# Decode attention block in fp32: output weights in two loads of 24 and 8 heads, the last values between them, all heads joined in one way, the mean taken from row sums

## Chip, core and metric

One core of a Trainium2 chip runs one launch of the kernel. The metric is the time on the device in microseconds. TensorE (PE), VectorE (DVE), ScalarE (ACT), GpSimd (POOL) and SyncE (SP) run their own instruction streams and wait for each other through semaphores; 16 DMA engines fill the on-chip memory.

## What is computed

One decode step, batch 2, model width 512, 32 heads of 128, a cache of 8192 keys and values for each head, all in fp32: a layer norm, attention over the cache with the output weights `wo`, the residual, a second layer norm, and a two-layer network with a squared ReLU.

```python
def _A_ref(x, k_cache, v_cache, wq, wo):
    q = (x @ wq).reshape(B, Sq, H, Dh).transpose(0, 2, 1, 3)
    scores = jnp.einsum("bhqd,bhkd->bhqk", q, k_cache) * (Dh ** -0.5)
    p = _softmax(scores, axis=-1)
    o = jnp.einsum("bhqk,bhkd->bhqd", p, v_cache)
    return o.transpose(0, 2, 1, 3).reshape(B, Sq, H * Dh) @ wo
...
h = x + _A_ref(_layernorm(x), k_cache, v_cache, wq, wo)
h2 = h + _B_ref(_layernorm(h), w1, b1, w2, b2)      # relu(z @ w1 + b1) ** 2 @ w2 + b2
```

## The kernel before

**Streaming.** The 64 pairs of head and batch element (pair number = 2 x head + batch element) are streamed through three buffers `ring[0..2]` of 8 MB, each holding a pair's keys (first half) and values (second half). All loads of this kind are issued by SP in program order (`load`, L122); SP waits for a semaphore `FREE` before it refills a buffer, and DVE gives it when it is through with the buffer. For each pair PE multiplies keys with the query (`front`, L234) into PSUM tiles `s[0..2]`, in two halves of 4096 keys; DVE takes maxima (`maxes`, stored negated in `nm`), ACT exponentials with their sums (`exps`, into `ls`), and DVE multiplies values with the exponentials and sums along the row (`product`, L252, eight a pair, into `ac`). Maxima are local to a partition row and a half; the rows are put on one scale at the end.

**The tail** (L139 on) begins when the last pair (63, so head 31 of batch element 1) is loaded. Its keys go into the first half of `ring[0]` with a semaphore of their own (`LK`). Then SP loads the output weights `WO` (8 MB, `ring[1]`) at once, the last values in five pieces (`V_PIECES`, in eighths), and, when `ring[2]` is free, `W1` in two pieces (three quarters and one quarter of its rows) and `W2` in four. `take` (L60) is the wait for a load, `after` (L54) the wait for another engine's result; a wait stands in the stream of the engine that waits, and everything behind it on that engine waits too.

**Joining.** `stats` (L287) gives each pair the minimum of its negated maxima over all rows and the factor `wt` for each of them, `sums` and `invert` the reciprocal of the softmax denominator `rl`, `folded` (L317) the weighted sum over the rows. In the kernel before this runs for 62 pairs (31 heads) first; DVE writes the joined outputs, each 16 times repeated, into `big` (L337), PE multiplies them with `WO` (L344, two passes a head, four column groups), ACT copies the sum into `acc` (L348), and PE folds the four groups and turns the result to features on partitions (L351). DVE's program has this order behind it: products 0 to 2 of the last pair, the addition of that result to `hT` (L366), a second `stats` for head 31, products 3 and 4, `sums`, product 5, `invert`, products 6 and 7. Then head 31 is joined alone: `folded`, `o31` (L379), PE with its block of `WO` (L382), an addition to `hT` (L385).

**The rest.** `centre` (L176) takes the mean over features with a DVE sum, a PE product with `ones_d` and a DVE subtraction into `xc`; `xr` (L387) is the input of W1, which PE multiplies in the order of its pieces (L396). After the first piece `spread` (L186) makes the variance and its root. DVE transposes the result, scales it, adds `b1` and squares; PE adds `h + b2` through the identity (L405) and W2's products (L421) into one PSUM tile, which DVE copies (L426) and SP stores (L428).

Of the kernel before, what the change touches and what calls it, by code (L numbers as in the profile page):

```python
# [27 lines left out]
W1_PIECES = [3, 1]  # L28
V_PIECES = [(0, 2), (2, 4), (4, 6), (6, 7), (7, 8)]
# [34 lines left out]
def attention_block_kernel(nc, small, kvd, wqd, kld, vld, wod, w1d, w2d, out):  # L64
# [32 lines left out]
    o31 = sbuf("o31", B)  # L97
    xr = sbuf("xr", DB, 16, B)
    hT = sbuf("hT", DB, B)
# [15 lines left out]
    SM, LK = p.sem("small"), p.sem("k63")  # L115
    LV = [p.sem(f"v63_{k}") for k in range(len(V_PIECES))]
# [59 lines left out]
    def centre(src, tok, bank):  # L176
        p.after("dve", tok)
        tok = p.tell("dve", dve.tensor_reduce(part, src.rearrange("p d b -> p b d"), axis=AX.X, op=ALU.add))  # L178
        p.after("pe", tok)
        tok = p.tell("pe", pe.matmul(bank[:, :B], ones_d, part, start=True, stop=True))  # L180
        p.after("dve", tok)
        tok = p.tell("dve", dve.tensor_tensor(xc, src, bank[:, None, :B].to_broadcast([P, DB, B]), op=ALU.subtract))
        p.after("dve", tok)
        return tok

    def spread(bank):  # L186
        tok = p.tell("dve", dve.tensor_tensor(sq, xc, xc, op=ALU.mult))
        p.after("dve", tok)
        tok = p.tell("dve", dve.tensor_reduce(part, sq.rearrange("p d b -> p b d"), axis=AX.X, op=ALU.add))
# [5 lines left out]
        tok = p.tell("dve", dve.reciprocal(rstd, rstd))  # L195
        return tok
# [3 lines left out]
    tok = centre(xT, t_c, pm[0])  # L200
    tok = spread(pm[1])
# [83 lines left out]
    t_m = p.tell("dve", dve.tensor_copy(hT, xT))  # L285

    def stats(lo, nb):  # L287
        n2 = slice(lo * NC, (lo + nb) * NC)
        p.after("pe", t_m)
        for j in range(NQ):  # L290
            ins = pe.matmul(pm[0][:, j * nb * NC : (j + 1) * nb * NC], pick[:, j, :], nm[:, n2], start=True, stop=True)  # L291
        tok = p.tell("pe", ins)
        p.after("dve", tok)
        tok = p.tell("dve", dve.tensor_reduce(gm[:, lo : lo + nb], pm[0][:, : NQ * nb * NC].rearrange(  # L294
            "p (j i c) -> p i j c", j=NQ, c=NC), axis=AX.XY, op=ALU.min))
        p.after("dve", tok)
        w3 = wt[:, n2].rearrange("p (i c) -> p i c", c=NC)
        tok = p.tell("dve", dve.tensor_tensor(w3, gm[:, lo : lo + nb, None].to_broadcast([P, nb, NC]),
                                              nm[:, n2].rearrange("p (i c) -> p i c", c=NC), op=ALU.subtract))
        p.after("act", tok)  # L300
        return p.tell("act", act.activation(wt[:, n2], wt[:, n2], AF.Exp))

    def sums(lo, nb, tok):
        n2 = slice(lo * NC, (lo + nb) * NC)
        p.after("dve", tok)
        tok = p.tell("dve", dve.tensor_tensor(lw[:, n2], ls[:, n2], wt[:, n2], op=ALU.mult))  # L306
        p.after("pe", tok)
        l3 = lw[:, n2].rearrange("p (i c) -> p i c", c=NC)
        for c in range(NC):
            ins = pe.matmul(pm[1][:, :nb], pick_all, l3[:, :, c], start=(c == 0), stop=(c == NC - 1))  # L310
        return p.tell("pe", ins)

    def invert(lo, nb, tok):
        p.after("dve", tok)
        return p.tell("dve", dve.reciprocal(rl[:, lo : lo + nb], pm[1][:, :nb]))

    def folded(lo, nb):  # L317
        aw4 = aw[:, lo * NC * NH : (lo + nb) * NC * NH].rearrange("p (i c e) -> p i c e", c=NC, e=NH)
        ac4 = ac[:, lo * NC * NH : (lo + nb) * NC * NH].rearrange("p (i c e) -> p i c e", c=NC, e=NH)
        w4 = wt[:, lo * NC : (lo + nb) * NC].rearrange("p (i c) -> p i c", c=NC)[:, :, :, None].to_broadcast([P, nb, NC, NH])  # L320
# [7 lines left out]
        return p.tell("pe", ins)  # L328

    tok = stats(0, NG)  # L330
    tok = sums(0, NG, tok)
    tok = invert(0, NG, tok)
    p.after("dve", tok)
    tok = folded(0, NG)
    p.after("dve", tok)
    o4 = big[:, : HG * 32].rearrange("p (h r b) -> p h r b", r=16, b=B)
    tok = p.tell("dve", dve.tensor_tensor(  # L337
        o4, pm[0][:, :NG].rearrange("p (h b) -> p h b", b=B)[:, :, None, :].to_broadcast([P, HG, 16, B]),
        rl[:, :NG].rearrange("p (h b) -> p h b", b=B)[:, :, None, :].to_broadcast([P, HG, 16, B]), op=ALU.mult))
    p.after("pe", tok)  # L340
    p.take(pe, LD[1], 16)
    for h in range(HG):
        j = h % NQ
        ins = pe.matmul(pm[1][32 * j : 32 * j + 32, :], big[:, h * 32 : h * 32 + 32], WO[:, h, :],  # L344
                        start=(h < NQ), stop=(h + NQ >= HG))
    tok = p.tell("pe", ins)
    p.after("act", tok)
    tok = p.tell("act", act.activation(acc, pm[1], AF.Copy))  # L348
    p.after("pe", tok)
    for d in range(DB):  # L350
        ins = pe.matmul(pm[0][:, d * B : (d + 1) * B], acc[:, d * P : (d + 1) * P], fold[:, :B], start=True, stop=True)  # L351
# [24 lines left out]
    p.after("dve", t_v)  # L376
    tok = folded(NG, B)
    p.after("dve", tok)
    tok = p.tell("dve", dve.tensor_tensor(o31, pm[0][:, :B], rl[:, NG:BH], op=ALU.mult))  # L379
    p.after("pe", tok)  # L380
    for d in range(DB):
        ins = pe.matmul(pm[1][:, d * B : (d + 1) * B], WO[:, H - 1, d * P : (d + 1) * P], o31, start=True, stop=True)  # L382
    tok = p.tell("pe", ins)
    p.after("dve", tok)
    tok = p.tell("dve", dve.tensor_tensor(hT, hT, pm[1][:, : DB * B].rearrange("p (d b) -> p d b", b=B), op=ALU.add))  # L385
# [77 lines left out]
```

## Time and profile before

| | us |
|---|---|
| median of 3 timed runs | 1309.69 (1308.71 to 1312.11) |
| the profiled execution, time on the device | 1312.31 |
| its span, first to last instruction | 1309.7 |
| DMA, HBM read | 561.00 MB, 428 GB/s over the span |
| busy in the span | PE 410.1, weight loads (PEld) 112.6, DVE 759.0, ACT 160.2 |
| mean granted TensorE clock | 0.647 of full |

Times in the profile are microseconds from the span's start. In timeline rows the columns are start, duration, engine, line, operation, output and inputs, count, and in brackets the idle time before it and what ended it; neighbouring instructions of one line are merged. Rows of the chain of waits have start, duration, engine, output, line, count. DMA rows give the time from the issue of a load to its landing; the issue's duration is that of SP's instruction alone. In rows of windows the busy time of PE, weight loads, DVE, ACT and POOL is followed by the granted clock (1 is full speed), the share of the DMA engines and GB/s.

### The profile page before, as it was taken

The page shows a single profiled execution, that of the slowest core. Times are in us where ns is not written, and L with a number is a line of the kernel's source. Part 1 is how long each engine was busy: PE and PEld are TensorE (multiplying, and loading weights), DVE is VectorE, ACT ScalarE, POOL GpSimd, SP SyncE. Part 2 cuts the span into 40 slices and gives each one's busy share as a digit, 9 for nine tenths or more (in the row PEclk, how much of TensorE's full clock was granted, in tenths as well). Part 3 has the DMA queues.
Part 4 walks back from the last instruction along what each step waited for, and adds up shares of the span by engine and source line. Part 5 has one row for each costly group of instructions (what it writes and reads, how often), then busy time and mean ns, then how long its engine had stood idle before and what let it go on. Part 6 is the DMA issues. An engine that isn't in the chain of part 4 may idle for free. (4 is left out here: it accounts for less than half of the span.)

```text
span 1309.7 us, 8250 instructions
## 1 busy us (share of the span) xinstructions
PE 410.1 (31%) x2390; PEld 112.6 (9%) x2390; DVE 759.0 (58%) x1227; ACT 160.2 (12%) x267; POOL 0.7 (0%) x6
## 2 busy tenths in 40 slices
PE   2323223323323323332331332332232233133156
PEld 0100000000000000000000000000000000000013
DVE  1465575565566466557556556655645755664663
ACT  0011011011111111101101111110110110111110
POOL 0000000000000000000000000000000000000000
PEclk9766566656666566656666666766666675666667
DMA  9999999999999999999999999999999999999996
GB/s 417 417 447 422 442 438 426 444 422 444 420 444 420 446 418 446 420 444 436 428 444 420 446 420 444 420 444 420 446 418 446 428 436 442 422 444 422 430 423 271
DMA packets 11381, 561.14 MB, mean 428 GB/s; under 512 B 1392, under 2 KB 1520, under 8 KB 2160
## 3 DMA queue, kind: packets, MB, share of 16 engines
q1 hardware_dynamic: 11232, 561.06, 99.1%
q8 instruction: 3, 0.05, 0.0%
q10 hardware_dynamic: 144, 0.01, 0.0%
q14 instruction: 2, 0.02, 0.0%
HBM read 561.00 MB, written 0.07 MB: 428 GB/s over the span
## 5 line engine op out<-in xcount | busy, mean ns | idle before, releaser
L239 PE MATMUL s<-ring,qc 128*32 128x512 f32 x2048 | 369.8, 888 | 852.0 <-PEq L61 852.0
L254 DVE SCALAR_TENSOR_TENSOR ring<-ring,s 128x1024 f32<-128x1024 f32 x512 | 589.5, 1217 | 3.7 <-DVEq L61 3.6
L245 DVE TENSOR_REDUCE nm<-s 128x1024 f32 (+1 forms) x128 | 156.7, 1225 | 488.4 <-DVEq L61 488.4
L249 ACT ACTIVATE s<-s,nm 128x1024 f32<-128x1024 f32 x128 | 139.3, 1088 | 1081.8 <-ACTq L61 1081.8
L239 PEld LDWEIGHTS s<-ring,qc 128*32 128x32 f32 x2048 | 93.0, 155 | 1128.5 <-issue 1128.5
L254 DVE DVE_READ_ACCUMULATOR ring<-ring,s (+1 forms) x512 | 42.5, 83 | 0.0
L249 ACT ACTIVATION_READ_ACCUMULATOR s<-s,nm (+1 forms) x128 | 24.7, 193 | 0.0
L178 DVE TENSOR_REDUCE part<-sm 128x2 f32<-128x8 f32 x1 | 0.2, 161 | 19.3 <-DVEq L61 19.3
L344 PE MATMUL pm<-ring,big 128*32 128x512 f32 x62 | 10.0, 798 | 2.4 <-PEq L61 2.4
L216 PE MATMUL s<-ring,xr 128*32 128x512 f32 x64 | 9.7, 773 | 2.3 <-issue 2.3
L180 PE MATMUL pm<-part,ones_d 128*128 128x2 f32 x4 | 1.2, 363 | 23.6 <-DVE part L178 23.6
L221 DVE STREAM_TRANSPOSE big<-s 128x512 f32<-128x512 f32 x2 | 1.4, 718 | 9.1 <-PE s L216 9.1
L396 PE MATMUL s<-ring,xr 128*32 128x448 f32 x32 | 5.9, 886 | 0.6 <-issue 0.6
L270 DVE COPY qc<-qs 128x96 f32 x21 | 5.1, 243 | 0.0
L195 DVE RECIPROCAL rstd<-rstd 128x2 f32<-128x2 f32 x2 | 0.3, 166 | 7.7 <-ACT rstd L193 7.7
L291 PE MATMUL pm<-nm,pick 128*128 128x124 f32 (+1 forms) x16 | 3.3, 357 | 4.5 <-DVE hT L285 4.3
L193 ACT ACT_TABLE_LOAD x1 | 1.3, 1283 | 25.1 <-PE pm L191 25.1
L421 PE MATMUL s<-ring,a 128*2 128x128 f32 x112 | 3.2, 272 | 1.3 <-issue 1.3
L310 PE MATMUL pm<-lw,pick_all 128*128 128x62 f32 (+1 forms) x8 | 2.1, 395 | 4.6 <-DVE lw L306 4.6
L344 PEld LDWEIGHTS pm<-ring,big 128*32 128x32 f32 x62 | 2.6, 139 | 9.1 <-issue 9.1
L366 DVE TENSOR_TENSOR hT<-hT,pm 128x8 f32<-128x8 f32 x1 | 0.2, 164 | 5.6 <-PE pm L351 5.6
L291 PEld LDWEIGHTS pm<-nm,pick 128*128 128x128 f32 x16 | 2.9, 271 | 5.7 <-DVE hT L285 5.4
(63 smaller groups left out, 37.1 us busy)
## 6 DMA issues: line engine op xcount, KB each, us to landing
ring<-in_kld SPq DMA_DIRECT2D x1, 4096.0 KB, 31.1
ring<-in_vld SPq DMA_DIRECT2D x3, 1024.0 KB, 36.3
ring<-in_w1d SPq DMA_DIRECT2D x1, 2688.0 KB, 28.7
ring<-in_w2d SPq DMA_DIRECT2D x1, 2048.0 KB, 35.1
ring<-in_vld SPq DMA_DIRECT2D x2, 512.0 KB, 39.7
ring<-in_w2d SPq DMA_DIRECT2D x1, 1024.0 KB, 34.1
ring<-in_kvd SPq DMA_DIRECT2D x63, 40.9
ring<-in_w1d SPq DMA_DIRECT2D x1, 896.0 KB, 30.5
```

The lines of the kernel that those rows point to most:

```text
L216: ins = pe.matmul(s[0][32 * j : 32 * j + 32, n * 512 : n * 512 + 512], xs[:, d, :], ring[2][:, c0 : c0 + 512], start=(d == 0), stop=(d == ...
L221: tok = p.tell("dve", dve.transpose(big[:, n * 512 : n * 512 + 512], s[0][:, n * 512 : n * 512 + 512]))
L239: ins = pe.matmul(s[k][32 * j : 32 * j + 32, n * 512 : (n + 1) * 512], qc[:, u, :], slot[:, c0 : c0 + 512], start=True, stop=True)
L245: dve.tensor_reduce(at(nm, pair, NC, c, 1), s[k], axis=AX.X, op=ALU.max, negate=True).then_inc(MAXED, 1)
L249: act.activation(s[k], s[k], AF.Exp, bias=at(nm, pair, NC, c, 1), scale=1.0, accum_out=at(ls, pair, NC, c, 1)).then_inc(EXPED, 1)
L254: return dve.scalar_tensor_tensor(v, v, 1.0, s[k], op0=ALU.mult, op1=ALU.mult, accum_out=at(ac, pair, NC * NH, c * NH + e, 1))
L270: dve.tensor_copy(qc, qs[:, bass.ds(i + 3, 3)][:, :, None].to_broadcast([P, 3, 32])).then_inc(QUERY, 1)
L291: ins = pe.matmul(pm[0][:, j * nb * NC : (j + 1) * nb * NC], pick[:, j, :], nm[:, n2], start=True, stop=True)
L310: ins = pe.matmul(pm[1][:, :nb], pick_all, l3[:, :, c], start=(c == 0), stop=(c == NC - 1))
L344: ins = pe.matmul(pm[1][32 * j : 32 * j + 32, :], big[:, h * 32 : h * 32 + 32], WO[:, h, :], start=(h < NQ), stop=(h + NQ >= HG))
L396: ins = pe.matmul(y[32 * j : 32 * j + 32, :], xs[:, d, :], W1[:, d, j * FQ : (j + 1) * FQ], start=(d == 0), stop=(d == DB - 1))
L421: ins = pe.matmul(o[32 * j : 32 * j + B, :], a2[:, m, :], W2[:, m, j * P : (j + 1) * P], start=False, stop=(m == FB - 1))
```

## The change

SP's order becomes: keys of the last pair, 24 heads of the output weights (6 MB), the values in three pieces (eighths 0 to 2, 3 to 5, 6 and 7), 8 heads of the output weights (2 MB, semaphore `LO`), W1 in two halves, W2 as before. The factors and denominators are computed once, for all 64 pairs, before the products of the last pair. Heads 0 to 30 are folded and joined, PE multiplies 24 of them with their weights, DVE does the eight products of the last pair in a row, head 31 is folded and joined in the same way as the others, and PE adds heads 24 to 31 to the same accumulators. ACT's copy into `acc` also sums each row; from these sums one PE product with `foldm` (`fold` divided by the width) gives the mean of the attention output over features. The centred `x` of the first layer norm, kept in `xc`, plus the attention output (`hc`), less that mean, is the input of W1. The squares for the variance and `hb` (now from `xb`, which holds `x + b2`) are issued ahead of W1, the rest of the variance after its first half.

```diff
-W1_PIECES = [3, 1]
-V_PIECES = [(0, 2), (2, 4), (4, 6), (6, 7), (7, 8)]
+W1_PIECES = [2, 2]
+V_PIECES = [(0, 3), (3, 6), (6, 8)]
+HA = 24
...
-    load(ring[1], wod, LD[1])
+    load(WO[:, :HA], wod[:, :HA], LD[1])
     for k, (a, b) in enumerate(V_PIECES):
         load(ring[0][:, HALF + a * CS : HALF + b * CS], vld[:, a * CS : b * CS], LV[k])
+    load(WO[:, HA:], wod[:, HA:], LO)
...
+    p.after("dve", t_c)
+    t_c = p.tell("dve", dve.tensor_scalar(foldm, fold[:, :B], 1.0 / D, None, op0=ALU.mult))
...
+    def squares(src, tok):
         p.after("dve", tok)
+        tok = p.tell("dve", dve.tensor_tensor(sq, src, src, op=ALU.mult))
         p.after("dve", tok)
+        return p.tell("dve", dve.tensor_reduce(part, sq.rearrange("p d b -> p b d"), axis=AX.X, op=ALU.add))
+
+    def root(bank, tok):
         p.after("pe", tok)
         tok = p.tell("pe", pe.matmul(bank[:, :B], ones_d, part, start=True, stop=True))
         p.after("act", tok)
         tok = p.tell("act", act.activation(rstd, bank[:, :B], AF.Sqrt, bias=eps_t, scale=1.0))
         p.after("dve", tok)
+        return p.tell("dve", dve.reciprocal(rstd, rstd))
...
-    t_m = p.tell("dve", dve.tensor_copy(hT, xT))
-
...
+
+    t_m = p.tell("dve", dve.tensor_tensor(xb, xT, b2T[:, :, None].to_broadcast([P, DB, B]), op=ALU.add))
+
+    def by_pair(t):
+        return t.rearrange("p (i c) -> p i c", c=NC)
+
+    p.after("pe", t_m)
+    for j in range(NQ):
+        ins = pe.matmul(pm[0][:, j * BH * NC : (j + 1) * BH * NC], pick[:, j, :], nm, start=True, stop=True)
+    tok = p.tell("pe", ins)
+    p.after("dve", tok)
+    tok = p.tell("dve", dve.tensor_reduce(gm, pm[0].rearrange("p (j i c) -> p i j c", j=NQ, c=NC), axis=AX.XY, op=ALU.min))
+    p.after("dve", tok)
+    tok = p.tell("dve", dve.tensor_tensor(by_pair(wt), gm[:, :, None].to_broadcast([P, BH, NC]), by_pair(nm), op=ALU.subtract))
+    p.after("act", tok)
+    tok = p.tell("act", act.activation(wt, wt, AF.Exp))
+    act.activation(warm, eps_t, AF.Sqrt)
+    t_z = p.tell("act", act.activation(s[2][:, :P], zero.to_broadcast([P, P]), AF.Copy))
+    p.after("dve", tok)
+    tok = p.tell("dve", dve.tensor_tensor(lw, ls, wt, op=ALU.mult))
+    p.after("pe", tok)
+    for c in range(NC):
+        ins = pe.matmul(pm[1][:, :BH], pick_all, by_pair(lw)[:, :, c], start=(c == 0), stop=(c == NC - 1))
+    tok = p.tell("pe", ins)
+    p.after("dve", tok)
+    t_l = p.tell("dve", dve.reciprocal(rl, pm[1][:, :BH]))
 
     def folded(lo, nb):
         aw4 = aw[:, lo * NC * NH : (lo + nb) * NC * NH].rearrange("p (i c e) -> p i c e", c=NC, e=NH)
         ac4 = ac[:, lo * NC * NH : (lo + nb) * NC * NH].rearrange("p (i c e) -> p i c e", c=NC, e=NH)
-        w4 = wt[:, lo * NC : (lo + nb) * NC].rearrange("p (i c) -> p i c", c=NC)[:, :, :, None].to_broadcast([P, nb, NC, NH])
+        w4 = by_pair(wt[:, lo * NC : (lo + nb) * NC])[:, :, :, None].to_broadcast([P, nb, NC, NH])
         tok = p.tell("dve", dve.tensor_tensor(aw4, ac4, w4, op=ALU.mult))
         p.after("dve", tok)
         as3 = acs[:, lo * NH : (lo + nb) * NH].rearrange("p (i e) -> p i e", e=NH)
...
         p.after("pe", tok)
         for e in range(NH):
             ins = pe.matmul(pm[0][32 * e : 32 * e + 32, :nb], fold, as3[:, :, e], start=True, stop=True)
-        return p.tell("pe", ins)
-
...
+        tok = p.tell("pe", ins)
+        p.after("dve", tok, t_l)
+        n = nb // B
+        return p.tell("dve", dve.tensor_tensor(
+            big[:, lo * 16 : (lo + nb) * 16].rearrange("p (h r b) -> p h r b", r=16, b=B),
+            pm[0][:, :nb].rearrange("p (h b) -> p h b", b=B)[:, :, None, :].to_broadcast([P, n, 16, B]),
+            rl[:, lo : lo + nb].rearrange("p (h b) -> p h b", b=B)[:, :, None, :].to_broadcast([P, n, 16, B]), op=ALU.mult))
+
+    def projected(lo, hi):
+        for h in range(lo, hi):
+            j = h % NQ
+            ins = pe.matmul(pm[1][32 * j : 32 * j + 32, :], big[:, h * 32 : h * 32 + 32], WO[:, h, :],
+                            start=(h < NQ), stop=(h + NQ >= H))
+        return ins
+
     tok = folded(0, NG)
-    p.after("dve", tok)
-    o4 = big[:, : HG * 32].rearrange("p (h r b) -> p h r b", r=16, b=B)
-    tok = p.tell("dve", dve.tensor_tensor(
-        o4, pm[0][:, :NG].rearrange("p (h b) -> p h b", b=B)[:, :, None, :].to_broadcast([P, HG, 16, B]),
-        rl[:, :NG].rearrange("p (h b) -> p h b", b=B)[:, :, None, :].to_broadcast([P, HG, 16, B]), op=ALU.mult))
     p.after("pe", tok)
     p.take(pe, LD[1], 16)
-    for h in range(HG):
-        j = h % NQ
-        ins = pe.matmul(pm[1][32 * j : 32 * j + 32, :], big[:, h * 32 : h * 32 + 32], WO[:, h, :],
-                        start=(h < NQ), stop=(h + NQ >= HG))
-    tok = p.tell("pe", ins)
-    p.after("act", tok)
-    tok = p.tell("act", act.activation(acc, pm[1], AF.Copy))
-    p.after("pe", tok)
-    for d in range(DB):
-        ins = pe.matmul(pm[0][:, d * B : (d + 1) * B], acc[:, d * P : (d + 1) * P], fold[:, :B], start=True, stop=True)
-    t_h = p.tell("pe", ins)
-
-
+    projected(0, HA)
     order = [(c, e) for c in range(NC) for e in range(NH)]
-    t_w = t_l = None
     piece = {a: k for k, (a, b) in enumerate(V_PIECES)}
     for n, (c, e) in enumerate(order):
         if e == 0:
...
         if n in piece:
             p.take(dve, LV[piece[n]], 16)
         ins = product(c, LAST, c, e, ring[0])
-        if n == 2:
-            p.after("dve", t_h)
-            t_h = p.tell("dve", dve.tensor_tensor(hT, hT, pm[0][:, : DB * B].rearrange("p (d b) -> p d b", b=B), op=ALU.add))
-            t_m = t_h
-            t_w = stats(NG, B)
-        if n == 4:
-            t_l = sums(NG, B, t_w)
-            act.activation(warm, eps_t, AF.Sqrt)
-        if n == 5:
-            t_l = invert(NG, B, t_l)
-    t_v = p.tell("dve", ins)
-    t_z = p.tell("act", act.activation(s[2][:, :P], zero.to_broadcast([P, P]), AF.Copy))
-    p.after("dve", t_v)
-    tok = folded(NG, B)
-    p.after("dve", tok)
-    tok = p.tell("dve", dve.tensor_tensor(o31, pm[0][:, :B], rl[:, NG:BH], op=ALU.mult))
-    p.after("pe", tok)
+    tok = p.tell("dve", ins)
+    p.after("dve", tok)
+    t_o = folded(NG, B)
+    p.take(pe, LO, 16)
+    projected(HA, HG)
+    p.after("pe", t_o)
+    tok = p.tell("pe", projected(HG, H))
+    p.after("act", tok)
+    tok = p.tell("act", act.activation(acc, pm[1], AF.Copy, accum_out=rows))
+    p.after("pe", tok)
+    h2 = pm[0][:, : DB * B]
     for d in range(DB):
-        ins = pe.matmul(pm[1][:, d * B : (d + 1) * B], WO[:, H - 1, d * P : (d + 1) * P], o31, start=True, stop=True)
-    tok = p.tell("pe", ins)
-    p.after("dve", tok)
-    tok = p.tell("dve", dve.tensor_tensor(hT, hT, pm[1][:, : DB * B].rearrange("p (d b) -> p d b", b=B), op=ALU.add))
-    tok = centre(hT, tok, pm[0])
-    tok = p.tell("dve", dve.tensor_copy(xr, xc[:, :, None, :].to_broadcast([P, DB, 16, B])))
-    p.after("pe", tok)
+        ins = pe.matmul(h2[:, d * B : (d + 1) * B], acc[:, d * P : (d + 1) * P], fold[:, :B], start=True, stop=True)
+    t_h = p.tell("pe", ins)
+    mean = s[2][:, 512 : 512 + B]
+    t_n = p.tell("pe", pe.matmul(mean, rows.to_broadcast([P, P]), foldm, start=True, stop=True))
+    h3 = h2.rearrange("p (d b) -> p d b", b=B)
+    p.after("dve", t_h)
+    tok = p.tell("dve", dve.tensor_tensor(hc, xc, h3, op=ALU.add))
+    p.after("dve", t_n, tok)
+    tok = p.tell("dve", dve.tensor_tensor(xr, hc[:, :, None, :].to_broadcast([P, DB, 16, B]),
+                                          mean[:, None, None, :].to_broadcast([P, DB, 16, B]), op=ALU.subtract))
+    p.after("pe", tok)
+    t_q = squares(xr[:, :, 0, :], tok)
+    t_b = p.tell("dve", dve.tensor_tensor(hb, xb, h3, op=ALU.add))
...
-            t_r = spread(pm[1])
-            t_b = p.tell("dve", dve.tensor_tensor(hb, hT, b2T[:, :, None].to_broadcast([P, DB, B]), op=ALU.add))
+            t_r = root(pm[1], t_q)
```

More of the change, by code (lines that the diff above doesn't have):

```diff
@@ L96, in attention_block_kernel @@
     acc = sbuf("acc", D)
-    o31 = sbuf("o31", B)
+    rows = sbuf("rows", 1)
+    foldm = sbuf("foldm", B)
+    xb = sbuf("xb", DB, B)
+    hc = sbuf("hc", DB, B)
     xr = sbuf("xr", DB, 16, B)
-    hT = sbuf("hT", DB, B)
     hb = sbuf("hb", DB, B)
@@ L115, in attention_block_kernel @@
     SM, LK = p.sem("small"), p.sem("k63")
+    LO = p.sem("wo_b")
     LV = [p.sem(f"v63_{k}") for k in range(len(V_PIECES))]
@@ L194, in spread @@
         p.after("dve", tok)
-        tok = p.tell("dve", dve.reciprocal(rstd, rstd))
-        return tok
+        return p.tell("dve", dve.reciprocal(rstd, rstd))
     p.after("act", t_c)
     p.take(dve, SM, 16)
-    tok = centre(xT, t_c, pm[0])
-    tok = spread(pm[1])
+    p.after("dve", t_c)
+    tok = p.tell("dve", dve.tensor_reduce(part, xT.rearrange("p d b -> p b d"), axis=AX.X, op=ALU.add))
+    p.after("pe", tok)
+    tok = p.tell("pe", pe.matmul(pm[0][:, :B], ones_d, part, start=True, stop=True))
+    p.after("dve", tok)
+    t_x = p.tell("dve", dve.tensor_tensor(xc, xT, pm[0][:, None, :B].to_broadcast([P, DB, B]), op=ALU.subtract))
+    tok = root(pm[1], squares(xc, t_x))
     p.after("dve", tok)
@@ L284, in attention_block_kernel @@
         maxes(c, LAST, c)
-    t_m = p.tell("dve", dve.tensor_copy(hT, xT))
[L287 to L291, printed above, removed]
-        tok = p.tell("pe", ins)
-        p.after("dve", tok)
[L294 to L299, printed above, removed]
-        p.after("act", tok)
-        return p.tell("act", act.activation(wt[:, n2], wt[:, n2], AF.Exp))
@@ L303, in sums @@
[L303 to L306, printed above, removed]
-        p.after("pe", tok)
-        l3 = lw[:, n2].rearrange("p (i c) -> p i c", c=NC)
-        for c in range(NC):
-            ins = pe.matmul(pm[1][:, :nb], pick_all, l3[:, :, c], start=(c == 0), stop=(c == NC - 1))
-        return p.tell("pe", ins)
-    def invert(lo, nb, tok):
-        p.after("dve", tok)
-        return p.tell("dve", dve.reciprocal(rl[:, lo : lo + nb], pm[1][:, :nb]))
+    t_m = p.tell("dve", dve.tensor_tensor(xb, xT, b2T[:, :, None].to_broadcast([P, DB, B]), op=ALU.add))
@@ L407, in attention_block_kernel @@
     tok = p.tell("dve", dve.transpose(yT, y))
-    p.after("dve", tok)
+    p.after("dve", tok, t_r)
     y3 = yT.rearrange("p (m r) -> p m r", r=32)
```

19 lines of the change are left out of this document (1 added, 18 removed).

## The prediction

> **What bounds the kernel now.** I read the page first: does one resource fill the span?
>
> ```profile
> span 1309.7 us, 8250 instructions
> DMA  9999999999999999999999999999999999999996
> ```
>
> The DMA engines are full in all slices but the last, so nothing outside the tail can pay while the bytes stay the same. Next, the SP timeline and the landing times behind it: when does each tail load arrive (issue start plus time to landing)?
>
> ```profile
> 1240.16 0.33 SPq L123 DMA_DIRECT2D ring<-in_wod  x1
> 1240.54 2.32 SPq L123 DMA_DIRECT2D ring<-in_vld  x5
> 1260.18 0.80 SPq L123 DMA_DIRECT2D ring<-in_w1d  x2
> 1261.02 14.11 SPq L123 DMA_DIRECT2D ring<-in_w2d  x4
> ...
> ring<-in_w2d SPq DMA_DIRECT2D x1, 2048.0 KB, 35.1
> ring<-in_w1d SPq DMA_DIRECT2D x1, 896.0 KB, 30.5
> ring<-in_wod SPq DMA_DIRECT2D x1, 32.2
> ...
> L123 SPq DMA_DIRECT2D ring<-in_vld x2: 431/432/432, 1242.0 to 1242.4; - x2
> DMA to landing us min/median/max: 39.3/39.7/40.1
> ...
> L123 SPq DMA_DIRECT2D ring<-in_w2d x2: 2102/2122/2143, 1270.8 to 1273.0; - x2
> DMA to landing us min/median/max: 26.9/27.6/28.4
> ```
>
> The output weights land at 1240.16 + 32.2 = 1272.4, the last values at 1242.4 + 40.1 = 1282.5, the end of W1 30.5 behind its second issue, about 1260.5, at 1291.0, the first W2 piece at 1296.1, its last at 1273.0 + 26.9 = 1299.9. The end is at 1309.7, so something other than the DMA ends last. The chain of waits says what:
>
> ```profile
> 1272.52 10.02 PE pm L344 x62
> 1282.55 0.61 ACT acc L348
> 1283.20 1.07 PE pm L351 x8
> 1293.12 1.88 PE pm L382 x8
> 1295.43 0.59 PE pm L180 x2
> 1296.59 4.71 PE s L396 x24
> 1301.81 1.16 PE s L396 x8
> 1304.46 3.28 PE s L421 x112
> 1307.77 0.29 DVE res L426
> ```
>
> It begins where the output weights land (1272.4 against 1272.52), works through 31 heads, then the rest of the values, head 31 alone, the mean, W1 (1296.59 to 1302.97) and W2, whose 112 matmuls run without a pause because the last piece has been there for 4.6 us. One window confirms that the transfers are over (last two columns: DMA share, GB/s) and shows a clock at half:
>
> ```profile
> 1300.00:1301.00 1.00, 1.00 (x8) 0.00 (x0) 0.00 (x0) 0.00 (x0) 0.00 (x0) 0.50 0.00 0
> ```
>
> So the tail has room for 1307.74 − 1299.9 = 7.8 us, less the work that the last W2 piece itself needs.
>
> **The change, part by part.** I follow the new order with the byte times above. The bytes and their FIFO order from the last keys to W2 are the same in total; there are 11 loads instead of 12.
>
> *Loads.* The last keys are there when their matmuls start, the following row; from it the 8 MB of output weights took 19.1 us, the 4 MB of values 10.1 (1272.4 to 1282.5).
>
> ```profile
> 1253.31 5.37 PE L239 MATMUL s<-ring,qc 128*32 128x512 f32 x32 [4.05 <-PEq L61]
> ```
>
> New: 24 heads are 6/8 of it, 1253.3 + 14.3 = 1267.6; values 0 to 2 (3/8 of 10.1) 1271.4, 3 to 5 1275.2, 6 and 7 1277.7; the last 8 heads at 1282.5 as the last values did; W1 in halves, (1291.0 − 1282.5)/2 each, 1286.8 and 1291.0; W2 unchanged. SP issues one load fewer before W1, and W2's four issues, during which SP is held 14.11 us, delay nothing else that SP has to do until the output. That the 48 KB and 16 KB rows are read out of 64 KB rows is not in the trace for this tensor; the nearest rows are the values, 8 KB or less out of 32 KB, at 2.5 us per MB against 2.4 for the contiguous output weights. Bounds: 0 to 8 × 0.1 = 0.8 us later. I take 0, since rows of 48 and 16 KB stand nearer to the contiguous ones.
>
> *Joining all heads at once.* DVE's order up to the joined outputs stays, over 64 pairs in place of 62.
>
> ```profile
> 1270.17 1.19 DVE L337 TENSOR_TENSOR big<-pm,rl 128x992 f32<-128x992 f32 x1 [0.56 <-PE pm L327]
> 1275.00 1.22 DVE L254 SCALAR_TENSOR_TENSOR ring<-ring,s 128x1024 f32<-128x1024 f32 x1 [3.64 <-DVEq L61]
> 1289.72 1.22 DVE L254 SCALAR_TENSOR_TENSOR ring<-ring,s 128x1024 f32<-128x1024 f32 x1
> 1290.87 1.22 DVE L254 SCALAR_TENSOR_TENSOR ring<-ring,s 128x1024 f32<-128x1024 f32 x1
> 1292.12 0.17 DVE L321 TENSOR_TENSOR aw<-ac,wt 128x16 f32<-128x16 f32 x1
> 1292.90 0.16 DVE L379 TENSOR_TENSOR o<-pm,rl 128x2 f32<-128x2 f32 x1 [0.41 <-PE pm L327]
> ```
>
> `big` is done at 1271.36, plus about 0.05 for the two pairs (2 in 62 of the few operations before it). The eight products now run in one train, one per 1.15 us (1289.72 to 1290.87); a piece that is waited for adds some 0.2 (PE's first matmul, 1272.52, was 0.15 behind its landing). First at 1271.6; the fourth waits for 1275.2 + 0.2; the eighth at 1275.4 + 4 × 1.15 = 1280.0; `aw` 1.25 later, 1281.25; from there to the joined output of head 31 was 1.0 (1292.12 to 1293.12), so 1282.3. The 24 heads on PE start at 1271.5 and end near 1280, beside the products. PE then waits twice: for the fold of head 31, behind which heads 24 to 30 queue, and for the last 8 heads' weights at 1282.5. The weights come 0.2 us later, so the fold wait costs nothing; were the products later, every microsecond past 0.2 would count. PE starts at 1282.65.
>
> *The last eight heads.* Their 16 passes depend on the clock (weight-load groups at half clock, called cold here, and at full, warm; then windows whose third column from the right is the granted clock):
>
> ```profile
> 1274.19 0.22 PEld L344 LDWEIGHTS pm<-ring,big 128*32 128x32 f32 x4 [0.63 <-issue]
> 1275.05 0.22 PEld L344 LDWEIGHTS pm<-ring,big 128*32 128x32 f32 x4 [0.63 <-issue]
> 1279.74 0.14 PEld L344 LDWEIGHTS pm<-ring,big 128*32 128x32 f32 x4 [0.29 <-issue]
> 1280.17 0.13 PEld L344 LDWEIGHTS pm<-ring,big 128*32 128x32 f32 x4 [0.29 <-issue]
> ...
> 1278.00:1278.50 0.50, 0.50 (x8) 0.04 (x4) 0.50 (x1) 0.00 (x0) 0.00 (x0) 0.56 0.96 393
> 1285.00:1285.50 0.50, 0.50 (x6) 0.50 (x5) 0.00 (x0) 0.00 (x0) 0.00 (x0) 0.77 1.50 645
> 1302.00:1302.50 0.50, 0.50 (x8) 0.07 (x4) 0.23 (x2) 0.11 (x1) 0.00 (x0) 0.66 0.00 0
> ```
>
> Four passes take 0.86 at half clock, 0.43 at full: 3.4 or 1.7 us, plus 0.4 until the last is out. The clock rose 6 us into the first train, fell 2.7 us behind its end, and rose again 5.7 us into W1. Here PE idles from about 1280.0 to 1282.65, 2.65 us: it can be either. Ends: 1286.5 cold, 1284.8 warm.
>
> *To W1.* ACT's copy, now with row sums: 0.61 and the reading of the accumulator, bounded by nothing and by its own mean, 0.19; I take 0.15, with 0.06 of handing over.
>
> ```profile
> L249 ACT ACTIVATION_READ_ACCUMULATOR s<-s,nm (+1 forms) x128 | 24.7, 193 | 0.0
> 26.89 0.29 DVE L203 TENSOR_TENSOR xr<-xc,rstd 128x128 f32<-128x128 f32 x1
> ```
>
> Then eight passes with `acc` (1.07 in the warm row L351, 1.88 in the cold row L382), two for the mean (0.59 cold, by the same ratio 0.34 warm), beside which `hc` fits, and `xr` by the row above with 0.06 of handing over, 0.35. Cold: 0.82 + 1.88 + 0.59 + 0.35 = 3.65, W1 at 1290.1. Warm: 2.6, W1 at 1287.4. The removed link from the end of L344 to W1 took 14.05 (1282.54 to 1296.59): a second set of maxima, five products behind it, head 31 alone, two additions and the mean over features.
>
> *W1 and W2.* W1 with its variance passes took 6.38; cold, it starts at 1290.1, needs the second half at 1293.2 (there since 1291.0), ends at 1296.5; then 1.49 to W2 (1302.97 to 1304.46) and 3.28: 1301.25. Warm, the second half begins with its landing, 1291.15; half of 6.38 later is 1294.3, W2 at 1295.8, and now the last piece rules: 1299.9 + 0.15 + 8 of 112 passes, 0.23: 1300.3. The matmuls so end at 1300.3 to 1301.25 against 1307.74: a gain of 6.5 to 7.4, and I take the middle, 6.9.
>
> *At nothing:* `foldm` stands at the start, where DVE sits idle before its first sum (its row follows); `xb` replaces the copy `hT`, one 128x8 operation for another; squares and `hb` run on DVE beside W1's first half, 3 us (uncovered: 0.2 each); the square-root warm-up and the zeroing go to ACT's idle time behind the weights' exponentials, before `acc`.
>
> ```profile
> L178 DVE TENSOR_REDUCE part<-sm 128x2 f32<-128x8 f32 x1 | 0.2, 161 | 19.3 <-DVEq L61 19.3
> ```
>
> *Clock rule.* The changes in the three windows fall, by the share of full speed in each, at 1278.44, 1285.27 and 1302.34: 6.8 and 17.1 us apart. The Trainium skill, page "TensorE: Matmul & The Clock Gate", section "Part 1: The HAM clock gate", says that busyness is judged in windows of 3.4 us that run on by themselves, one busy window giving full and one idle window half clock. The trace agrees: 2 and 5 windows. By that rule alone the pause at 1280 could fall on either side in each execution, which leaves the sum between the same two ends; its other result is rival B.
>
> **Rivals.** *B: the clock is still at half in W2.* A train of 6.4 us as in W1 may miss a rise, or the wait for W1's second half may break it. For it: the fall at 1285.3 with PE at work on narrow matmuls. Against: W1's train of the same length got the rise before W2. Price: 3.28 once more behind the cold chain, 1304.5 against 1307.74, a gain of 3.2: 1306.5.
>
> *C, slower: the split output weights load slowly.* All later loads queue behind them. The forecast's gain is gone when the 8 MB take 6.9 us more, 26 instead of 19.1; from there on the time is above 1309.69, at half the rate 1302.8 + 19.1 = 1321.9. Against: the values, also pieces of power-of-two rows, at 2.5 us per MB. The Trainium skill, "DMA: Bandwidth & Descriptors", section "Latency and other measured facts", has loads of 16 KB rows falling from 214 to 164 GB/s at a row pitch of 2 MB; by that ratio the 19.1 would be 24.9 and the gain 1.1. No run here shows such a pitch; here it is 64 KB.
>
> *D: the reordering does not take effect,* because loads issued within 2.3 us share the engines and the values arrive only with everything, at 1282.5. Then eight products end in `aw` at 1282.65 + 7 × 1.15 + 1.25 = 1291.95, head 31 is joined at 1293.0, and the cold path (3.8 + 3.65) starts W1 at 1300.4, 3.8 behind the 1296.59 of now: 1313.5. Against: the five value pieces, issued together, let the products begin at 1275.00, 7.5 us before the last landed.
>
> **How the numbers follow.** The profiled execution took 1312.31 us on the device, 2.6 outside its span; the timed median is 1309.69, 2.6 lower. I carry the tail's gain over whole: 1309.69 − 6.9 = 1302.8. Chances: forecast 0.82, B 0.11, C 0.04, D 0.03. The forecast's own range is 1300.8 to 1304.5 (6.5 to 7.4, W2 partly at half clock, and the runs' spread from 1308.71 to 1312.11); below it, a last piece that lands 1 us earlier gives 1300.3, above it B ends the range at 1306.5. A change of 0.3% or 3.9 us is about what a measurement of this kernel can tell from none: the forecast is faster, B within it, C slower, and D, which lies on that edge, is halved: 0.82, 0.125, 0.055.
>
> **What would show it.** PE's first train starting at the end of `big` rather than at a landing; eight products without a stop, ending near 1281; the last eight heads starting at a landing near 1282.5; W1 between 1287 and 1290; W2's matmuls with pauses before their last pieces, or ending within 1.5 us of the last landing. Wrong would be W1 later than 1293, a last W2 landing past 1301, or a W2 train of over 5 us without waits.

## The result, and the profile after

| | before | changed |
|---|---|---|
| median us (first comparison, 5 runs each) | 1309.82 (1308.71 to 1312.11) | 1303.72 (1303.55 to 1304.72) |
| ratio, 95% interval | | 0.995 [0.9939, 0.9961] |
| profiled execution, span | 1309.7 | 1301.9 |
| profiled execution, time on the device | 1312.31 | 1303.67 |

6.1 us are gone; 6.9 were forecast. The page of the changed kernel, in the places that answer to those shown of before:

```profile
span 1301.9 us, 8206 instructions
DMA  9999999999999999999999999999999999999998
...
PE s L410 0%; DVE res L415 0%
```

The DMA engines are now busy into the last slice, and the chain of waits has shrunk to W2 (L410) and the copy of the result. In order of time it is this (start, duration, what):

```profile
1298.31 0.04 issue
1298.35 1.66 PE s L410 x48
1300.01 0.02 issue
1300.04 0.29 DVE res L415
```

It begins at 1298.31: before, it reached back to the landing of the output weights at 1272.5. The 48 matmuls are W2's last three pieces (6 of 14 blocks, 8 passes each); what releases 1298.35 is the landing of the second piece, at 1298.2. The timeline shows how the tail got there:

```profile
1271.30 1.22 DVE L258 SCALAR_TENSOR_TENSOR ring<-ring,s 128x1024 f32<-128x1024 f32 x1
1271.38 7.25 PE L338 MATMUL pm<-ring,big 128*32 128x512 f32 x48 [1.36 <-issue]
1279.56 1.22 DVE L258 SCALAR_TENSOR_TENSOR ring<-ring,s 128x1024 f32<-128x1024 f32 x1
1281.55 0.19 DVE L330 TENSOR_TENSOR big<-pm,rl 128x32 f32<-128x32 f32 x1 [0.37 <-PE pm L326]
1282.36 3.45 PE L338 MATMUL pm<-ring,big 128*32 128x512 f32 x16 [0.87 <-PEq L62]
1286.61 1.05 PE L366 MATMUL pm<-fold,acc 128*128 128x2 f32 x8 [0.81 <-ACT acc L362]
1288.36 2.75 PE L386 MATMUL s<-ring,xr 128*32 128x448 f32 x16 [0.48 <-issue]
1291.56 2.06 PE L386 MATMUL s<-ring,xr 128*32 128x448 f32 x16
1295.83 1.93 PE L410 MATMUL s<-ring,a 128*2 128x128 f32 x64 [2.00 <-PEq L62]
1298.35 1.62 PE L410 MATMUL s<-ring,a 128*2 128x128 f32 x48 [0.59 <-PEq L62]
```

The reader sees two trains side by side from 1271.3 on, DVE's eight products (first and last are shown) and PE's 24 heads; then the last eight heads at 1282.36, W1 at 1288.36 instead of 1296.59, and W2 in two parts with waits ahead of both. `PEq` as the releaser of the last two is PE's own sequencer sitting in the wait for a load. The loads (issue, and time to landing of the W2 piece that lands last):

```profile
1240.21 0.33 SPq L127 DMA_DIRECT2D ring<-in_wod  x1
1242.01 0.43 SPq L127 DMA_DIRECT2D ring<-in_wod  x1
...
ring<-in_wod SPq DMA_DIRECT2D x1, 6144.0 KB, 27.3
ring<-in_wod SPq DMA_DIRECT2D x1, 2048.0 KB, 40.2
...
L127 SPq DMA_DIRECT2D ring<-in_w2d x1: 3183/3183/3183, 1266.7 to 1266.7; - x1
DMA to landing us min/median/max: 32.7/32.7/32.7
```

24 heads land at 1267.5, the other 8 at 1282.2, the last of W2 at 1266.7 + 32.7 = 1299.4. PE's last matmul ends at 1300.01, 0.6 behind it; before, that distance was 7.8. In this execution the tail's own work is no longer what ends last.

### The profile page after: what moved, and what is told of

Its sections match the earlier page's. It is cut to its first block, busy times and chain, and to the rows that moved or that the text cites. A ratio compares the mean times of both kernels' runs of the same rounds, so it can differ in the third digit from the quotient of the medians.

```text
span 1301.9 us, 8206 instructions
## 1 busy us (share of the span) xinstructions
PE 412.5 (32%) x2372; PEld 109.2 (8%) x2372; DVE 757.7 (58%) x1221; ACT 160.1 (12%) x267; POOL 0.7 (0%) x6
## 5 line engine op out<-in xcount | busy, mean ns | idle before, releaser
L243 PE MATMUL s<-ring,qc 128*32 128x512 f32 x2048 | 376.8, 903 | 845.2 <-PEq L62 845.2
L410 PE MATMUL s<-ring,a 128*2 128x128 f32 x112 | 3.5, 272 | 2.6 <-PEq L62 2.6
```

The lines of the kernel that those rows point to most:

```text
L243: ins = pe.matmul(s[k][32 * j : 32 * j + 32, n * 512 : (n + 1) * 512], qc[:, u, :], slot[:, c0 : c0 + 512], start=True, stop=True)
L410: ins = pe.matmul(o[32 * j : 32 * j + B, :], a2[:, m, :], W2[:, m, j * P : (j + 1) * P], start=False, stop=(m == FB - 1))
```

## Experiments

Two theories. *Joining:* the time went because DVE's last products no longer wait for PE's first train, and head 31 has no path of its own. *Order:* it went because the last values land 5 us earlier, 1277.3 instead of 1282.5. And for the end: is W2's landing the bound, or still the chain of work? Each comparison has its own runs of before on the same chip: median 1310.35 for the first four runs, 1310.38 for the next four, 1310.46 for the last two.

### The kernel before, once more

> The kernel before, once more, nothing left out. The changed kernel's five runs have times 1.7 to 1.8 us above their spans (1303.67 against 1301.9); the profiled execution of before had 1312.31 against 1309.7. If that execution was only a long one, this run shows a span near 1308 for a time near 1309.8, and its tail as before: output weights landing near 1272, their 62 passes 10 us, W1 14 us behind them, last W2 landing near 1299 and the matmuls' end 7 to 8 us behind that. If instead the time outside the span differs between the two kernels, the span stays near 1307 for 1309.8. Either way the ratio is 1.000 within 0.1%.

1310.81 (11 runs), ratio 1.000 [0.9991, 1.0009]. Its spans run from 1307.6 to 1310.3; those of before beside it (16 runs) have a median of 1308.7. So the execution that the prediction was made from, span 1309.7, was a long one by 1.0 us. The time outside the span is 1.3 to 1.4 in most runs of before, 2.6 was rare, and it is 1.7 to 1.8 in all five of the changed kernel. In spans the change is worth 1308.7 − 1302.0 = 6.7 us; 0.4 of that comes back outside.

### Order alone

```diff
-    load(ring[1], wod, LD[1])
+    load(WO[:, :HA], wod[:, :HA], LD[1])
...
+    load(WO[:, HA:], wod[:, HA:], LO)
...
     for h in range(HG):
+        if h == HA:
+            p.take(pe, LO, 16)
```

> The kernel before with the output weights in two loads of 24 and 8 heads and the values (still five pieces) between them; joining, mean and W1 pieces as before. Theory 1, the gain comes from the joining (DVE's last products no longer wait for PE's 31 heads, and head 31 has no path of its own): here PE has 24 heads done near 1280, waits for the last weights until about 1282.3, does 7 heads at half clock and ends near 1285.7 instead of 1282.5; DVE still waits there behind its third product; the rest follows unchanged, so the time is about 3 us longer than before, 1313 (1311 to 1314). Theory 2, the gain comes from the values landing 5 us earlier: most of the 6 us show here, 1304 to 1306.

1314.49 (6 runs), ratio 1.0032 [1.002, 1.0045]: slower by 4.1, and 0.5 above the range that was expected if joining is the cause. The timeline of this kernel (L349 the heads, L371 the addition to `hT`, L257 a product, L401 W1):

```profile
1271.68 7.11 PE L349 MATMUL pm<-ring,big 128*32 128x512 f32 x48 [1.36 <-issue]
1273.77 1.22 DVE L257 SCALAR_TENSOR_TENSOR ring<-ring,s 128x1024 f32<-128x1024 f32 x1
1282.82 3.23 PE L349 MATMUL pm<-ring,big 128*32 128x512 f32 x14 [4.03 <-PEq L62]
1287.84 0.16 DVE L371 TENSOR_TENSOR hT<-hT,pm 128x8 f32<-128x8 f32 x1 [12.85 <-PE pm L356]
1289.49 1.21 DVE L257 SCALAR_TENSOR_TENSOR ring<-ring,s 128x1024 f32<-128x1024 f32 x1
1300.04 4.71 PE L401 MATMUL s<-ring,xr 128*32 128x448 f32 x24 [0.56 <-issue]
```

The third product starts at 1273.77, the fourth at 1289.49. The values were there (the last landed at 1277.8), and DVE stood idle for 12.85 us behind `PE pm L356`. Landing data earlier is worth nothing while the engine that uses them waits for something else, and that something was made later by the same order.

### Joining alone

```diff
-W1_PIECES = [2, 2]
-V_PIECES = [(0, 3), (3, 6), (6, 8)]
-HA = 24
+W1_PIECES = [3, 1]
+V_PIECES = [(0, 2), (2, 4), (4, 6), (6, 7), (7, 8)]
+HA = HG
...
-    load(WO[:, :HA], wod[:, :HA], LD[1])
+    load(WO, wod, LD[1])
...
-    load(WO[:, HA:], wod[:, HA:], LO)
...
-    p.take(pe, LO, 16)
-    projected(HA, HG)
```

> The changed kernel with the loads of before: output weights in one load ahead of the values, five pieces of values, W1 in three quarters and one; all heads joined alike, mean from row sums. PE does 31 heads at 1272.4 to 1282.4, the eight products follow the landings and end near 1284.8, head 31 is joined near 1285.9 and through PE at 1286.7, W1 starts at 1289.3 to 1290.3, W2's matmuls end at 1300.0 to 1301.5. Theory 1: 1303.7 to 1305.2, so at least three quarters of the gain. Theory 2 (the order is what counts): at least 1307.

1305.05 (5 runs), ratio 0.9953 [0.9939, 0.9967], 5.3 us of gain with the loads of before. W1 began later than expected:

```profile
1286.12 1.91 PE L336 MATMUL pm<-ring,big 128*32 128x512 f32 x2 [0.32 <-DVE big L328]
1288.81 1.87 PE L362 MATMUL pm<-fold,acc 128*128 128x2 f32 x8 [0.78 <-ACT acc L358]
1291.53 4.51 PE L382 MATMUL s<-ring,xr 128*32 128x448 f32 x24 [0.43 <-issue]
```

Two passes of head 31 alone took 1.91 us where the expectation had 0.8. Four passes in 0.86 at half clock, as the prediction counts them, is the rate of heads that alternate over four column groups; a lone head has one group, and that this is why it is slow is my reading of the two rows. The changed kernel, which ends with eight heads, does not pay it.

### One wait taken out of the kernel before

```diff
-    p.after("dve", tok)
+    t_l = invert(NG, B, sums(NG, B, stats(NG, B)))
+    act.activation(warm, eps_t, AF.Sqrt)
+    p.after("dve", t_l)
     tok = folded(0, NG)
...
         ins = product(c, LAST, c, e, ring[0])
-        if n == 2:
-            p.after("dve", t_h)
-            t_h = p.tell("dve", dve.tensor_tensor(hT, hT, pm[0][:, : DB * B].rearrange("p (d b) -> p d b", b=B), op=ALU.add))
-            t_m = t_h
-            t_w = stats(NG, B)
-        if n == 4:
-            t_l = sums(NG, B, t_w)
-            act.activation(warm, eps_t, AF.Sqrt)
-        if n == 5:
-            t_l = invert(NG, B, t_l)
     t_v = p.tell("dve", ins)
+    p.after("dve", t_h)
+    t_h = p.tell("dve", dve.tensor_tensor(hT, hT, pm[0][:, : DB * B].rearrange("p (d b) -> p d b", b=B), op=ALU.add))
```

> The kernel before with one wait taken away: maxima, sums and denominator of head 31 are worked out ahead of the products, and the addition of PE's result for 31 heads to hT stands behind the eighth product instead of the third. Head 31 keeps its own path and the mean is the old one; the loads are those of before. Theory 1 says that this wait of DVE is the largest part: products end near 1284.8, head 31 is joined near 1285.7, its 8 passes end near 1287.8, then two additions, the mean and the copy, W1 at 1289.7, W2's matmuls end near 1300.9: 1304 to 1305.5, about five of the six microseconds. Theory 2: no more than 1 us, 1309. Third view, the separate path and the mean are the larger part: 1306 to 1308.

1303.91 (5 runs), ratio 0.9951 [0.9938, 0.9965]: the whole measured gain, with the loads, the separate path and the mean of before. The wait that the edit takes out of the row of products has two parts, and the timeline of the kernel before shows the size of each, between its third product, which ends at 1278.7, and its fourth:

```profile
1284.29 0.16 DVE L366 TENSOR_TENSOR hT<-hT,pm 128x8 f32<-128x8 f32 x1 [5.59 <-PE pm L351]
1285.76 0.17 DVE L294 TENSOR_REDUCE gm<-pm 128x2 f32<-128x16 f32 x1 [1.30 <-PE pm L291]
1286.05 1.22 DVE L254 SCALAR_TENSOR_TENSOR ring<-ring,s 128x1024 f32<-128x1024 f32 x1
```

DVE waits 5.59 us for PE's result for 31 heads and 1.30 us for head 31's maxima, which stood behind that result and are now worked out ahead of the products. In the timeline of the edited kernel the products follow the landings, the last starts at 1283.34 instead of 1290.87, and PE waits for weights (the last three rows are from the chain of waits):

```profile
1283.34 1.22 DVE L254 SCALAR_TENSOR_TENSOR ring<-ring,s 128x1024 f32<-128x1024 f32 x1
1288.87 4.71 PE L389 MATMUL s<-ring,xr 128*32 128x448 f32 x24 [1.43 <-PEq L61]
...
1299.75 0.39 PE s L414 x4
1300.13 0.35 issue
1300.48 0.41 PE s L414 x4
```

W1 starts 0.14 behind the landing of its first piece, 1288.73 (1.43 behind `PEq`), and W2's last piece, landed at 1299.61, starts at 1299.75. So this kernel, too, meets the landings. The 0.35 before the last four matmuls is no such wait, since it lies within that last piece; with the order alone there are 0.24 at the same place, though the weights had been there for 11 us. Its cause stays open.

### That, with the new order

To the edit just shown comes that of the loads, with PE's wait ahead of head 24 as in the order alone:

```diff
-    load(ring[1], wod, LD[1])
+    load(WO[:, :HA], wod[:, :HA], LD[1])
...
+    load(WO[:, HA:], wod[:, HA:], LO)
```

> The kernel before with the wait taken away as in e3_before_products_free and the loads ordered as in e1_order_only (24 heads, five pieces of values, 8 heads). It asks what joining head 31 with the others is worth once the order of loads is changed. The products end near 1281, but heads 24 to 30 start at 1282.5 and PE's result for 31 heads reaches hT only near 1288 (1287.84 in e1_order_only); behind it come the fold of head 31 (1.0), its 8 passes (1.1 to 1.9), two additions and the mean (1.4), so W1 starts at 1291.5 to 1292.5 against 1288.36 in the changed kernel, and W2's matmuls end at 1302.7 to 1304: 1306 to 1307.5. If the separate path is worth nothing, 1303.7 to 1304.3, as e3_before_products_free.

1304.83 (5 runs), ratio 0.9959 [0.9945, 0.9973]: between the two figures, 1.1 above the changed kernel, and outside both. I had missed that working out head 31's factors ahead of the rest delays `big`, whose row and PE's below show it, by 3.9 us against 1270.09 in the changed kernel; PE's train then runs through the landing of the last weights without a stop and without losing its clock, and W1 starts at 1290.96.

```profile
1273.97 1.19 DVE L342 TENSOR_TENSOR big<-pm,rl 128x992 f32<-128x992 f32 x1 [0.56 <-PE pm L330]
1275.26 9.38 PE L351 MATMUL pm<-ring,big 128*32 128x512 f32 x62 [1.36 <-issue]
1290.96 3.75 PE L394 MATMUL s<-ring,xr 128*32 128x448 f32 x24 [0.56 <-issue]
1301.16 0.39 PE L419 MATMUL s<-ring,a 128*2 128x128 f32 x4 [0.54 <-issue]
```

With that order the changed kernel, with factors for all heads at once and one accumulation, is about 1 us faster, a difference of medians whose intervals overlap. Half of it is the pause of 0.54 in the last row, in which PE waits for nothing that the profile shows (the last weights landed at 1299.98). That joining in one accumulation is worth 1 us is therefore not shown.

### The mean, and the pieces

```diff
-    tok = p.tell("act", act.activation(acc, pm[1], AF.Copy, accum_out=rows))
+    tok = p.tell("act", act.activation(acc, pm[1], AF.Copy))
...
-    t_n = p.tell("pe", pe.matmul(mean, rows.to_broadcast([P, P]), foldm, start=True, stop=True))
...
+    tok = p.tell("dve", dve.tensor_reduce(part, hc.rearrange("p d b -> p b d"), axis=AX.X, op=ALU.add))
+    p.after("pe", tok)
+    t_n = p.tell("pe", pe.matmul(mean, ones_d, part, start=True, stop=True))
```

> The changed kernel with the mean taken over features again (a DVE sum of hc, a PE product with ones_d, then xr); ACT's copy sums no rows. Theory, the changed kernel's end is set by W2's landings (1295.7, 1298.2, 1298.8, 1299.4): W1 starts about 0.6 us later than 1288.36 and W2's first matmul, which waited 0.7 us for its weights, takes that up: time the same within 0.3 us, 1303.4 to 1304.2. If the chain of work still set the end, the 0.6 us would be seen.

1303.92 (5 runs), ratio 0.995 [0.9937, 0.9964]. W1 started at 1288.74, 0.4 later than in the changed kernel, and nothing of it is seen.

```diff
-W1_PIECES = [2, 2]
-V_PIECES = [(0, 3), (3, 6), (6, 8)]
+W1_PIECES = [3, 1]
+V_PIECES = [(0, 2), (2, 4), (4, 6), (6, 7), (7, 8)]
```

> The changed kernel with five pieces of values and W1 in three quarters and one. The values' pieces land no later than they are used (first at 1271, one per 1.15 us used, 2.5 us per two landed: the products end within 0.3 us of 1280.8); the first three quarters of W1 land near 1288.7 instead of 1286.5, 0.3 behind W1's start at 1288.36. W2's landings stay, so the time stays within 0.3 us: 1303.4 to 1304.2. If the pieces carried a part of the gain, it shows as more than 0.5 us.

1303.58 (5 runs), ratio 0.995 [0.9937, 0.9964]: no part of the gain either. Its profiled execution (1304.32) went another way, though: the granted clock was 0.50 from 1284 to 1290, W1 began late, and W2 ran through.

```profile
1290.12 4.71 PE L386 MATMUL s<-ring,xr 128*32 128x448 f32 x24 [0.42 <-issue]
1297.65 3.24 PE L410 MATMUL s<-ring,a 128*2 128x128 f32 x112 [1.26 <-PEq L62]
```

Here the chain of work ended last, 0.9 later than in the execution of the changed kernel shown above: which of the two ends last can differ between executions.

### Is W2's landing the bound?

More work on the chain, ahead of W1:

```diff
     p.after("dve", t_h)
+    for n in range(4):
+        t_x = p.tell("dve", product(1, LAST, 1, n, ring[0]))
+    p.after("dve", t_x)
```

> The changed kernel with four of the last pair's products done once more on DVE between PE's turned result and hc: 4 x 1.15 = 4.6 us put on the chain of work ahead of W1, nothing on the DMA. Theory, W2's landings set the end and the chain has 1 to 2 us to spare: W2 would start near 1299.6 instead of 1295.83 and run through in 3.3, ending near 1302.9 against 1300.0: 2.5 to 3.6 us longer, 1306.2 to 1307.3. Chain alone: 4.6 us longer, 1308.3. DMA alone: no change.

1307.3 (7 runs), ratio 0.9973 [0.9962, 0.9984]: 3.6 longer for 4.6 put in, the upper end of what was expected; in spans it is 4.0 (median 1306.0 against 1302.0). W2 now runs through in one piece:

```profile
1293.43 3.05 PE L389 MATMUL s<-ring,xr 128*32 128x448 f32 x16 [5.17 <-issue]
1299.92 3.24 PE L413 MATMUL s<-ring,a 128*2 128x128 f32 x112 [1.27 <-issue]
```

Fewer bytes with the same work: this kernel leaves out the load of the last eight heads' output weights and uses those of heads 0 to 7 in their place, so its result is not that of the task.

```diff
-    load(WO[:, HA:], wod[:, HA:], LO)
...
-    p.take(pe, LO, 16)
...
-            ins = pe.matmul(pm[1][32 * j : 32 * j + 32, :], big[:, h * 32 : h * 32 + 32], WO[:, h, :],
+            ins = pe.matmul(pm[1][32 * j : 32 * j + 32, :], big[:, h * 32 : h * 32 + 32], WO[:, h % HA, :],
```

> The changed kernel without the load of the last 8 heads' output weights (2 MB): these heads use the weights of heads 0 to 7, so all later landings come 4.8 us sooner with the work unchanged. It asks how far the chain of work stands behind the DMA. By the trace, heads 24 to 30 start at 1281.5 behind the fold of head 31, W1 at 1286.3 to 1287.6, and with nothing left to wait for W2 starts 6.4 to 7.9 later and ends 3.3 after that, 1296.3 to 1298.8 against 1300.0: time 1300.0 to 1302.5, 1 to 4 us gained. If only the DMA counted, all 4.8 us would be gained: 1298.9. If the chain already set the end, no more than 0.8 us (the earlier start of the last heads): 1303.

1301.68 (5 runs, 1299.67 to 1303.03), ratio 0.9934 [0.992, 0.9947]: 2.0 of the 4.8 us gained. Both bounds lie close together: in its profiled execution the landings end the changed kernel, and by these two runs the chain of work has 0.6 (in spans) to 2 us to spare. That is why a part of the added products and more than half of the saved bytes showed no effect.

### PE kept busy

```diff
     projected(0, HA)
+    for h in range(10):
+        j = h % NQ
+        pe.matmul(s[2][32 * j : 32 * j + 32, 512:], big[:, h * 32 : h * 32 + 32], WO[:, h, :], start=True, stop=True)
```

> The changed kernel with 20 more passes on PE, into a free PSUM tile, behind the first 24 heads, so that PE is not idle while DVE ends its products (in the profile idle from 1278.6 to 1282.36 but for the fold, clock down to half at 1282.07). Theory: the granted clock stays at full through the last 8 heads, whose 16 passes take 2.1 instead of 3.45 us, W1 starts 1 to 1.5 us sooner, and the time stays the same within 0.3 us because W2's landings set the end. If the half clock is what costs, 1302.2 to 1302.7.

1304.36 (5 runs, 1303.71 to 1304.84), ratio 0.9951 [0.9937, 0.9964]. The last eight heads did run at full clock, 1.92 us, and W1 began at 1287.44. But:

```profile
1289.08 0.38 PE L191 MATMUL pm<-part,ones_d 128*128 128x2 f32 x2
1291.55 2.23 PE L389 MATMUL s<-ring,xr 128*32 128x448 f32 x16 [2.08 <-PEq L62]
1296.46 4.67 PE L413 MATMUL s<-ring,a 128*2 128x128 f32 x112 [2.26 <-PEq L62]
...
1292.00:1293.00 1.00, 1.00 (x16) 0.46 (x12) 0.00 (x0) 0.00 (x0) 0.00 (x0) 0.81 1.08 459
1296.00:1298.00 2.00, 1.54 (x32) 1.14 (x36) 0.00 (x0) 0.00 (x0) 0.00 (x0) 0.50 0.95 372
```

PE was through W1's first half so early that it waited 2.08 us for the second; the clock (third from the right) fell in 1292 to 1293, was at half when W2 began, and W2 took 4.67 instead of the 3.28 of before, ending at 1301.13. This is rival B, brought about by finishing early: in this execution 1.1 us later than the changed kernel. The medians are 0.6 apart, where 0.3 at most was expected, with overlapping runs, so only the lack of a gain is certain.

## Why the prediction was right, point by point

*What bounds.* That the tail's chain ended last, 7.8 us behind the last transfer, and that W2's landing would be the next bound, held: the chain of waits is now W2 and the copy alone, and putting work in or taking bytes out moved the time by less than its own amount on either side.

*Landings.* 1267.5 for 24 heads (forecast 1267.6), 1282.2 for the other 8 (1282.5), 1299.4 for the last of W2 (1299.9). The cost of the split rows, taken as nothing between 0 and 0.8, was nothing, so C fell; the products began with the first piece, so D did. The 2 MB of the last eight heads took 4.9 us (1277.3 to 1282.2), 2.4 us per MB as the contiguous weights did. C's page, the Trainium skill's "DMA: Bandwidth & Descriptors", section "Latency and other measured facts", has its figures from copies between two HBM tensors at row pitches of 512 KiB and more; no slow-down of its kind appeared in these loads at a pitch of 64 KB.

*Joining.* `big` at 1271.28, the last product at 1279.56 (1280.0), head 31 joined at 1281.74 (1282.3), so the weights did land behind it. The forecast took 14.05 us between the first train and W1 as one link; the experiments split it. The largest part, enough for all of the measured gain, is that DVE no longer waits behind its third product, 5.59 us for PE's result and 1.30 for head 31's maxima. The mean from row sums and the sizes of the pieces add nothing that can be seen, and the order of loads costs 4.1 us by itself. What the joint accumulation is worth where that order stands is not settled: about 1 us lies between the medians, half of it a pause without a known cause.

*The clock.* The last eight heads ran at half, 3.45 us, but what followed ran at full: from their end at 1285.81 to W1 at 1288.36 it took 2.55 instead of the cold 3.65. The 0.4 that the sum adds for the last pass to come out is not seen: four times 0.86 is already 3.44. I had bounded the sum by all cold and all warm, and the end of the matmuls, 1300.01, fell 0.3 below the warm end because the last piece landed 0.5 sooner.

*The size.* 6.1 instead of 6.9. Two terms were mis-sized, in opposite directions. In the profiled executions the end of the matmuls moved by 7.7 (1307.74 to 1300.01), above the 6.5 to 7.4 of the sum. And the carrying over of one execution to the median, "I carry the tail's gain over whole", with the same time outside the span, took away more than this added: the profiled execution's span was 1.0 above the median of before, and the changed kernel spends 0.4 more outside its span. What that 0.4 is stays open: the kernel with four more products, otherwise the same program, has 1.3 again. That the forecast came within 0.8 is thus in part luck, since the two errors offset each other.

## What to carry to other kernels

When a chain of waits alternates between two engines, look in the program order of the waiting engine for work that needs nothing from the other and stands behind the wait: here, moving one addition back, and the work that stood behind it ahead, gave as much as the whole rewrite. An earlier landing is worth something only if its user is free at that time, so order of loads and order of use have to be changed together. When the tail has come down to the last landing, further shortening of its work is not seen, and an engine that gets there early may pay for the wait with its clock.

## What the runs showed of the hardware

The granted clock of TensorE changed at regular times. Windows of the changed kernel around each change (granted clock third from the right):

```profile
1275.00:1275.50 0.50, 0.50 (x11) 0.06 (x4) 0.50 (x1) 0.00 (x0) 0.00 (x0) 0.75 1.21 508
1282.00:1282.50 0.50, 0.14 (x4) 0.17 (x8) 0.00 (x0) 0.00 (x0) 0.00 (x0) 0.57 1.08 459
1285.00:1285.50 0.50, 0.50 (x8) 0.00 (x0) 0.00 (x0) 0.00 (x0) 0.00 (x0) 0.51 0.88 373
1288.50:1289.00 0.50, 0.50 (x8) 0.17 (x7) 0.23 (x2) 0.00 (x0) 0.00 (x0) 0.90 1.21 508
1292.00:1292.50 0.50, 0.50 (x8) 0.13 (x4) 0.12 (x1) 0.00 (x0) 0.00 (x0) 0.69 1.15 492
```

By the share of full speed in each they lie at 1275.25, 1282.07, 1285.49, 1288.90 and 1292.31: 6.82, 3.42, 3.41 and 3.41 us apart. From 1285.5 the clock turned over three times running, each time in line with what PE had done in the 3.4 us before. It ran at half while PE worked on the eight heads (1282.36 to 1285.81) and rose as they ended. In the 3.41 us at full that followed, PE spent 0.3 us on these heads and 0.5 us on W1; the rest was waiting and ten matmuls of two columns (L366, L369), and the clock fell. After 3.41 us of work on W1 it rose again. The Trainium skill, "TensorE: Matmul & The Clock Gate", section "Part 1: The HAM clock gate", gives such a window as 3413 ns, running on by itself; the trace agrees. I had not expected that one short train could so fall out of step with its clock.

The transfers do not end at once. In the changed kernel they fade over the last 2 us:

```profile
1297.00:1298.00 1.00, 0.76 (x28) 0.47 (x20) 0.00 (x0) 0.00 (x0) 0.00 (x0) 1.00 0.59 211
1298.00:1299.00 1.00, 0.65 (x24) 0.67 (x28) 0.00 (x0) 0.00 (x0) 0.00 (x0) 1.00 0.14 53
```

211 and then 53 GB/s (last column) against 431 over the span, and a landing waits for the slowest part: of the 16 completions that the trace has for the last piece of W2, twelve come between 1297.7 and 1298.2, four later, the last at 1299.43. That some of the 16 engines finish later than others is my reading of it. Where the landings end the kernel, this is the bound; whether it can be levelled was not tried.
